# Retention in chunks of 128 rows and FFN tiles of 512 tokens, in place of 96 and 384

## The chip, the cores and the metric

The kernel runs on one NeuronCore of a Trainium2 chip. The metric is the device time of one launch in microseconds (us); lower is better. A core has five engines that run side by side and wait for one another through semaphores: TensorE (PE in the profile; PEld are its weight loads), VectorE (DVE), ScalarE (ACT), GpSimd (POOL) and SyncE (SP), which here only issues loads.

## What is computed

The inputs q, k and v have 8 batches of 8 heads, 576 positions and 64 features. Retention is causal linear attention with a decay gamma that differs by head. Its output, 4608 tokens of 512 features, goes through a feed-forward network (FFN) that takes the greatest of three products and then multiplies once more. All of it is float32.

```python
scores = scale * np.matmul(q, k.transpose(0, 1, 3, 2))
gamma = 1.0 - 2.0 ** (-5.0 - np.arange(H, dtype=np.float32))
Dmat = np.where(rel >= 0, gamma[:, None, None] ** rel[None, :, :], 0.0)
attn_out = np.matmul(scores * Dmat[None, :, :, :], v)
x = attn_out.transpose(0, 2, 1, 3).reshape(B * S, H * D)     # 4608 x 512
h = np.maximum(np.maximum(x @ w1, x @ w2), x @ w3)           # 4608 x 768
return h @ w_out                                             # 4608 x 512
```

## The kernel before

Retention works on chunks of C = 96 positions of one batch, all 8 heads at once: 6 chunks to a sequence of 576, 48 chunks in all. A head's 64 features fill half of the 128 partitions, so heads go in 4 pairs. One chunk g is worked on in three steps, each of which is a "slot" of the main loop:

- `transposes(g)`: 4 transposes of the decayed keys (tile `kt`) and 4 of the queries (`qt`), copied to SBUF by DVE (`kT`) and ACT (`qT`).
- `scores(g)`: 8 products of keys and queries (tile `s`), one for each head, two of them at a time on the two halves of the array's rows; DVE multiplies them by the causal mask (`st`). Then 4 products `kv`, keys by values with 128 columns for a pair of heads, which DVE adds to the running state (`ssum`) and POOL multiplies by the decay (`state`). The last chunk of a sequence has no `kv`, since nothing follows it.
- `values(g)`: 8 products of the values and `st` (tile `o`), two at a time on the two halves of the array's columns, and 4 products of the state and the queries (`o<-qT,state`), which the first chunk of a sequence does without. DVE multiplies the sum by the output's decay and writes it into `xT`, feature-major.

In float32 each product other than a transpose is two MATMUL instructions in the trace. POOL multiplies the keys of chunk g by their decay in `decay_keys(g)` (tile `kd`), two chunks ahead; SP loads k, q and v of a chunk four chunks ahead (`load`).

The FFN works on tiles of NT = 4 C = 384 tokens, 12 tiles in all, one tile behind the retention. Its pieces of work are called atoms: 18 `up` (three weights by six blocks of 128 hidden features; each is four products of 128x128 weights with `NT` columns) and NT / 128 `down` (128 tokens by 512 features; six products of 512 columns). ACT copies the first of three `up` results into `h`, DVE takes the maximum with the others; ACT copies `down` into `osb` and issues the store.

What sets the order is the program text: each engine runs its instructions in the order in which the loop issues them. After each slot, as many atoms are issued as a credit allows, so that the atoms of one tile spread evenly over the 12 slots of the next tile's four chunks:

```python
slots_per_tile = 3 * CPT
atoms_per_tile = 3 * NF + NT // P
def slot(fn):
    fn()
    if todo:
        credit += atoms_per_tile
    while todo and credit >= slots_per_tile:
        credit -= slots_per_tile
        atom()
```

With CPT = 4 chunks to a tile, the FFN of the first tile is queued when `values(3)` has been issued; until then PE has retention alone. The weights arrive as the bits of float64 numbers and have to be converted: 24 pieces, each with five instructions on DVE (`expo`, `expo`, `frac`, `mant`, `expo`), two on ACT and one on POOL. Four pieces are converted beside chunks 0 and 1. The other 20 are issued two at a time ahead of each of the first ten atoms, so that on DVE two conversions stand ahead of whatever follows the atom's products. The products of `up` and `down` share two PSUM buffers, so `up` number n + 2 waits until ACT or DVE has read number n.

Of the kernel before, what the change touches and what calls it, by code (L numbers as in the profile page):

```python
"""Retention (decayed causal linear attention), then a maxout FFN, in float32.

Retention runs over chunks of C positions.  With positions counted within a chunk,
gamma^(i-j) = gamma^i * gamma^-j, so the keys carry gamma^-j, the outputs gamma^i / sqrt(D),
and what earlier chunks add is their state: S' = gamma^C * (S + K'^T V).  Its output comes out
feature-major, as the FFN's first products take it.  The FFN runs on tiles of NT tokens, each
while the retention of the next tile is worked out.
"""
# [10 lines left out]
FP32 = mybir.dt.float32  # L19
# [4 lines left out]
ALU = mybir.AluOpType  # L24
PSUM = bass.MemoryType.PSUM

C = 96
NT = 4 * C
AHEAD = 4
WAHEAD = 4  # L30
# [3 lines left out]
def kernel(  # L34
# [14 lines left out]
    nc = tc.nc  # L49
    P = 128  # L50
    B, H, S, D = q.shape
    N, DM = out.shape
    DF = moe_w1.shape[1]
    NP = H // 2
    NCH = S // C
    NG = B * NCH
    NDC = DM // P
    NF = DF // P
    CPT = NT // C
    assert S % C == 0 and N % NT == 0 and NT % P == 0 and 2 * D == P and NP == NDC  # L60

    const = ctx.enter_context(tc.tile_pool(name="const", bufs=1))
    wraw = ctx.enter_context(tc.tile_pool(name="wraw", bufs=WAHEAD))
# [2 lines left out]
    kpool = ctx.enter_context(tc.tile_pool(name="kpool", bufs=4))  # L66
    att = ctx.enter_context(tc.tile_pool(name="att", bufs=3))
    stp = ctx.enter_context(tc.tile_pool(name="stp", bufs=3))
    xpool = ctx.enter_context(tc.tile_pool(name="xpool", bufs=3))
    hpool = ctx.enter_context(tc.tile_pool(name="hpool", bufs=2))  # L70
    opool = ctx.enter_context(tc.tile_pool(name="opool", bufs=4))
    ps_t = ctx.enter_context(tc.tile_pool(name="ps_t", bufs=1, space=PSUM))
    ps_s = ctx.enter_context(tc.tile_pool(name="ps_s", bufs=1, space=PSUM))
    ps_o = ctx.enter_context(tc.tile_pool(name="ps_o", bufs=1, space=PSUM))
# [13 lines left out]
    causal = const.tile([C, C], FP32, name="causal")  # L88
# [1 line left out]
    nc.gpsimd.affine_select(out=causal[:], in_=causal[:], compare_op=ALU.is_ge, fill=0.0,  # L90
                            base=0, channel_multiplier=-1, pattern=[[1, C]])

# [1 line left out]
    raws, kds, qks, sts, states = {}, {}, {}, {}, {}  # L94

    def load(g):
        b, c = divmod(g, NCH)
        for n, src in (("k", k), ("q", q), ("v", v)):
            t = raws[n, g] = raw.tile([C, H, D], FP32, tag=n, name=n + "raw")
            nc.sync.dma_start(t[:], src[b, :, c * C:(c + 1) * C, :].rearrange("h p d -> p h d"))  # L100

    def decay_keys(g):
        t = kds[g] = kpool.tile([C, H, D], FP32, tag="kd", name="kd")
        nc.gpsimd.tensor_tensor(t[:], raws.pop(("k", g))[:], gk[:].unsqueeze(2).to_broadcast([C, H, D]),  # L104
                                op=ALU.mult)

    def pair(t, p):
        return t[:, 2 * p:2 * p + 2, :].rearrange("a h d -> a (h d)")

    def transposes(g):  # L110
        both = {}
        for n, src in (("k", kds[g]), ("q", raws.pop(("q", g)))):
            pt = ps_t.tile([P, NP, C], FP32, tag=n + "t", name=n + "t")
            for p in range(NP):
                nc.tensor.transpose(pt[:, p, :], pair(src, p), ident[:C, :C])  # L115
            t = both[n] = att.tile([P, NP, C], FP32, tag=n + "T", name=n + "T")
            if n == "k":
                nc.vector.tensor_copy(t[:], pt[:])  # L118
            else:
                nc.scalar.copy(t[:], pt[:])  # L120
        qks[g] = both

    def scores(g):
        c = g % NCH
        qT, kT = qks[g]["q"], qks[g]["k"]
        s = [ps_s.tile([C, NP, C], FP32, tag=f"s{j}", name=f"s{j}") for j in range(2)]
        for p in range(NP):
            for j in range(2):
                r = slice(D * j, D * (j + 1))
                nc.tensor.matmul(s[j][:, p, :], lhsT=kT[r, p, :], rhs=qT[r, p, :], start=True, stop=True)  # L130
        st = sts[g] = att.tile([C, 2, NP, C], FP32, tag="st", name="st")
        for j in range(2):
            nc.vector.tensor_tensor(st[:, j], s[j][:], causal[:].unsqueeze(1).to_broadcast([C, NP, C]),  # L133
                                    op=ALU.mult)
        kd = kds.pop(g)
        if c == NCH - 1:
            return
        kv = ps_kv.tile([P, NP, P], FP32, tag="kv", name="kv")
        for p in range(NP):
            nc.tensor.matmul(kv[:, p, :], lhsT=pair(kd, p), rhs=pair(raws["v", g], p), start=True, stop=True)  # L140
        t = states[g + 1] = stp.tile([P, NP, P], FP32, tag="state", name="state")
        if c == 0:
            nc.vector.tensor_tensor(t[:], kv[:], gs[:], op=ALU.mult)
        else:
            u = stp.tile([P, NP, P], FP32, tag="sum", name="ssum")
            nc.vector.tensor_tensor(u[:], kv[:], states[g][:], op=ALU.add)  # L146
            nc.gpsimd.tensor_tensor(t[:], u[:], gs[:], op=ALU.mult)  # L147
# [1 line left out]
    xT = {}  # L149

    def values(g):
        c = g % NCH
        t, i = divmod(g, CPT)
        if i == 0:
            xT[t] = xpool.tile([P, NDC, NT], FP32, tag="xT", name="xT")
        st, vr, qT = sts.pop(g), raws.pop(("v", g)), qks.pop(g)["q"]
        o = ps_o.tile([P, NP, C], FP32, tag="o", name="o")
        for p in range(NP):
            for j in range(2):
                nc.tensor.matmul(o[D * j:D * (j + 1), p, :], lhsT=vr[:, 2 * p + j, :], rhs=st[:, j, p, :],  # L160
                                 start=(p == 0), stop=(c == 0 and p == NP - 1), skip_group_check=True)
        if c > 0:
            sd = states.pop(g)
            for p in range(NP):
                nc.tensor.matmul(o[:, p, :], lhsT=sd[:, p, :], rhs=qT[:, p, :],  # L165
                                 start=False, stop=(p == NP - 1), skip_group_check=True)
        nc.vector.tensor_tensor(xT[t][:, :, i * C:(i + 1) * C], o[:], gq[:], op=ALU.mult)  # L167

# [1 line left out]
    # The weights come as the bits of float64 numbers, high word (sign, 11 bits of exponent, 20 of  # L170
    # mantissa) and low word (32 of mantissa).  As float32, rounded once:
    #   sign 2^(e - 1023) * ((1 + low 2^-52) + high's mantissa 2^-20),
    # with the exponent clamped to float32's, 0 below and infinity above.
    one = const.tile([P, 1], FP32, name="one")
    nc.vector.memset(one[:], 1.0)
    rebias = const.tile([P, 1], FP32, name="rebias")
# [4 lines left out]
    w_sb, bits = {}, {}  # L181
# [60 lines left out]
    def push_ffn(t):  # L242
        h = hpool.tile([P, NF, NT], FP32, tag="h", name="h")
        for fb in range(NF):
            for i in range(3):
                todo.append(lambda fb=fb, i=i: up(t, h, fb, i))
        for m in range(NT // P):
            todo.append(lambda m=m: down(t, h, m))

# [1 line left out]
    slots_per_tile = 3 * CPT  # L251
    atoms_per_tile = 3 * NF + NT // P
    credit = 0
# [1 line left out]
    def slot(fn):  # L255
        nonlocal credit
# [6 lines that stand above are left out]
# [9 lines left out]
    for g in range(2, AHEAD):  # L272
        load(g)
    decay_keys(0)
    decay_keys(1)
    transposes(0)
    for g in range(NG + 1):
        if g + AHEAD < NG:
            load(g + AHEAD)
        if g + 2 < NG:  # L280
            decay_keys(g + 2)
        if g + 1 < NG:
            slot(lambda: transposes(g + 1))
        if g > 0:
            slot(lambda: values(g - 1))
            if g % CPT == 0:
                push_ffn(g // CPT - 1)
        if g < NG:
            slot(lambda: scores(g))
        if g < 2:  # L290
            next_weights(2)
# [7 lines left out]


def _decays(H, D):
    """The decays of a chunk of C positions, constants of the shapes: for the keys [C, H], the outputs
    [2 D, H / 2, C] and the states [2 D, H / 2, 2 D], two heads to a block of the diagonal."""
    import numpy as _np

    gamma = 1.0 - 2.0 ** (-5.0 - _np.arange(H))
    pos = _np.arange(C)
    keys = gamma[None, :] ** -pos[:, None]
    outs = (gamma[:, None] ** pos[None, :] / math.sqrt(D)).reshape(H // 2, 2, C)
    outs = _np.repeat(outs.transpose(1, 0, 2), D, axis=0)  # L310
    states = _np.zeros((2, D, H // 2, 2, D))
    for j in range(2):
        states[j, :, :, j, :] = (gamma[j::2] ** C)[None, :, None]
    states = states.reshape(2 * D, H // 2, 2 * D)
    return {n: _np.ascontiguousarray(a, dtype=_np.float32)
            for n, a in (("key_decay", keys), ("out_decay", outs), ("state_decay", states))}
# [28 lines left out]
```

## Time and profile before

| what | value |
|---|---|
| three runs | 1023.16 us median, 1019.09 to 1024.40 |
| span of the profiled execution, first to last instruction | 1022.5 us |
| instructions | 11136 |
| granted TensorE clock, mean | 0.985 |
| DMA traffic | 51.51 MB |

The time that belongs to the profiled execution alone isn't listed; its span lies 0.7 us below the median of the runs, and that difference stands here for what lies around a span. The profile's page divides the span into 40 slices, lists groups of instructions by line and tile, and follows the chain of work that ended last back from the end. In a timeline, a row that ends in x16 is a run of 16 like instructions; since matmuls overlap and their ends are modelled, what one matmul costs is read from the distance between starts, not from its duration.

### The profile page before, as it was taken

How to read it: one execution, taken by the hardware profiler on the slowest of the kernel's cores; microseconds unless marked ns; L12 is line 12 of the kernel's file. 1: busy time of each engine (PE TensorE's matmuls, PEld its weight loads, DVE VectorE, ACT ScalarE, POOL GpSimd, SP SyncE). 2: the span in 40 equal slices, each digit the busy share in tenths (PEclk: the TensorE clock that was granted, in tenths of full speed). 3: DMA queues.
4: the chain of work that ended last, by engine and by line, in shares of the span. 5: the costliest groups of instructions: out<-in, count | busy, mean ns of one | idle time of the engine just before them, and what ended most of it. 6: DMA issues, size and time to landing. Idle time of an engine off the chain costs nothing.

```text
span 1022.5 us, 11136 instructions
## 1 busy us (share of the span) xinstructions
PE 977.8 (96%) x4720; PEld 596.4 (58%) x4720; DVE 284.8 (28%) x498; ACT 112.2 (11%) x205; POOL 122.4 (12%) x112
## 2 busy tenths in 40 slices
PE   5976599999999999999999999999999999999998
PEld 4843365665665665665665665665566566565554
DVE  4599921221221221220221221221222121121010
ACT  2133301001000000000100000000100100100100
POOL 2343310010010100110000100110010100000000
PEclk9988799999999999999999999999999999999999
DMA  9744612212212112121112112112112200000000
GB/s 234 157 126 146 142 24 55 47 24 54 47 24 54 33 39 54 24 47 44 35 40 50 35 25 56 44 24 57 44 24 44 57 8 9 24 1 1 31 1 31
DMA packets 128897, 51.51 MB, mean 50 GB/s; under 512 B 114000, under 2 KB 123344, under 8 KB 128848
## 3 DMA queue, kind: packets, MB, share of 16 engines
q1 hardware_dynamic: 123264, 40.91, 18.3%
q10 hardware_dynamic: 5584, 9.90, 3.0%
q8 instruction: 37, 0.61, 0.3%
q14 instruction: 12, 0.10, 0.0%
HBM read 41.36 MB, written 9.44 MB: 50 GB/s over the span
## 4 chain that ended last, share of the span: by engine, by line
PE 90%; DVE 7%; DMA 1%; SPq 1%; issue 1%; POOL 0%; ACT 0%; DVEq 0%
PE up L226 52%; PE down L236 18%; PE kv L140 4%; PE o L165 4%; PE s L130 4%; PE o L160 4%; DVE expo L203 2%; PE kt L115 2%; PE qt L115 1%; DVE expo L210 1%; DVE expo L202 1%; DVE mant L208 1%; DMA kraw<-in_k_dram 1%; DVE frac L207 1%; SPq L100 1%
## 5 line engine op out<-in xcount | busy, mean ns | idle before, releaser
L226 PE MATMUL up<-xT,w 128*128 128x384 f32 x1728 | 593.4, 496 | 27.1 <-DVE h L231 19.3
L226 PEld LDWEIGHTS up<-xT,w 128*128 128x128 f32 x1728 | 323.4, 193 | 233.4 <-issue 34.2
L231 DVE TENSOR_TENSOR h<-h,up 128x384 f32<-128x384 f32 x144 | 79.7, 554 | 401.6 <-PE up L226 396.7
L236 PE MATMUL down<-wout,h 128*128 128x512 f32 x432 | 189.3, 593 | 0.0
L236 PEld LDWEIGHTS down<-wout,h 128*128 128x128 f32 x432 | 81.3, 190 | 96.0 <-issue 92.8
L147 POOL TENSOR_TENSOR state<-ssum,gs 128x512 f32<-128x512 f32 x32 | 40.7, 1273 | 728.9 <-DVE ssum L146 721.9
L133 DVE TENSOR_TENSOR st<-s,causal 96x384 f32<-96x384 f32 x96 | 48.9, 548 | 143.8 <-PE s L130 143.8
L229 ACT COPY h<-up 128x384 f32<-128x384 f32 x72 | 34.4, 478 | 495.5 <-PE up L226 493.5
L167 DVE TENSOR_TENSOR xT<-o,gq 128x384 f32<-128x384 f32 x48 | 26.7, 556 | 105.1 <-PE o L165 103.5
L130 PEld LDWEIGHTS s<-qT,kT 64*96 64x96 f32 x768 | 39.6, 173 | 27.1 <-issue 27.1
L104 POOL TENSOR_TENSOR kd<-kraw,gk 96x512 f32<-96x512 f32 x48 | 50.0, 1052 | 13.9 <-DMA kraw<-in_k_dram 13.9
L160 PEld LDWEIGHTS o<-st,vraw 96*64 96x64 f32 x768 | 35.5, 144 | 27.0 <-issue 18.7
L140 PE MATMUL kv<-vraw,kd 96*128 96x128 f32 x320 | 50.9, 307 | 0.0
L165 PE MATMUL o<-qT,state 128*128 128x96 f32 x320 | 47.9, 296 | 0.0
L130 PE MATMUL s<-qT,kT 64*96 64x96 f32 x768 | 47.9, 268 | 0.0
L239 ACT COPY osb<-down 128x512 f32<-128x512 f32 x36 | 21.1, 586 | 220.5 <-PE down L236 220.5
L140 PEld LDWEIGHTS kv<-vraw,kd 96*128 96x128 f32 x320 | 42.8, 208 | 4.1 <-issue 0.9
L160 PE MATMUL o<-st,vraw 96*64 96x96 f32 x768 | 45.0, 262 | 0.0
L165 PEld LDWEIGHTS o<-qT,state 128*128 128x128 f32 x320 | 41.2, 201 | 5.0 <-issue 0.7
L118 DVE COPY kT<-kt 128x384 f32<-128x384 f32 x48 | 26.6, 554 | 56.9 <-PE kt L115 56.8
L115 PEld LDWEIGHTS kt<-ident,kd 96*128 96x128 f32 x192 | 23.1, 153 | 28.9 <-POOL kd L104 15.2
L115 PE MATMUL kt<-ident,kd 96*128 96x96 f32 x192 | 26.5, 264 | 14.0 <-POOL kd L104 14.0
(25 smaller groups left out, 251.8 us busy)
## 6 DMA issues: line engine op xcount, KB each, us to landing
kraw<-in_k_dram SPq DMA_DIRECT2D x48, 192.0 KB, 3.9
qraw<-in_q_dram SPq DMA_DIRECT2D x48, 192.0 KB, 4.1
vraw<-in_v_dram SPq DMA_DIRECT2D x48, 192.0 KB, 3.3
bits<-in_moe_w_dram SPq DMA_DIRECT2D x18, 512.0 KB, 3.8
out_dram<-osb ACTq DMA_DIRECT2D x36, 256.0 KB, 2.0
bits<-in_moe_w_out_dram SPq DMA_DIRECT2D x6, 512.0 KB, 3.5
gs<-in_state_decay_dram ACTq DMA_DIRECT2D x1, 256.0 KB, 5.3
gq<-in_out_decay_dram ACTq DMA_DIRECT2D x1, 192.0 KB, 4.1
```

Of the source, the lines that this page charges most:

```text
L104: nc.gpsimd.tensor_tensor(t[:], raws.pop(("k", g))[:], gk[:].unsqueeze(2).to_broadcast([C, H, D]), op=ALU.mult)
L115: nc.tensor.transpose(pt[:, p, :], pair(src, p), ident[:C, :C])
L130: nc.tensor.matmul(s[j][:, p, :], lhsT=kT[r, p, :], rhs=qT[r, p, :], start=True, stop=True)
L133: nc.vector.tensor_tensor(st[:, j], s[j][:], causal[:].unsqueeze(1).to_broadcast([C, NP, C]), op=ALU.mult)
L140: nc.tensor.matmul(kv[:, p, :], lhsT=pair(kd, p), rhs=pair(raws["v", g], p), start=True, stop=True)
L147: nc.gpsimd.tensor_tensor(t[:], u[:], gs[:], op=ALU.mult)
L160: nc.tensor.matmul(o[D * j:D * (j + 1), p, :], lhsT=vr[:, 2 * p + j, :], rhs=st[:, j, p, :], start=(p == 0), stop=(c == 0 and p == NP - 1) ...
L165: nc.tensor.matmul(o[:, p, :], lhsT=sd[:, p, :], rhs=qT[:, p, :], start=False, stop=(p == NP - 1), skip_group_check=True)
L226: nc.tensor.matmul(ps[:, 0:NT], lhsT=w_sb[i, fb][:, dc * P:(dc + 1) * P], rhs=xT[t][:, dc, :], start=(dc == 0), stop=(dc == NDC - 1))
L229: nc.scalar.copy(h[:, fb, :], ps[:, 0:NT])
L231: nc.vector.tensor_tensor(h[:, fb, :], h[:, fb, :], ps[:, 0:NT], op=ALU.max)
L236: nc.tensor.matmul(ps[:], lhsT=h[:, fb, m * P:(m + 1) * P], rhs=w_sb["out", fb][:], start=(fb == 0), stop=(fb == NF - 1))
```

## The change

C becomes 128, and with it NT = 4 C becomes 512: 36 chunks and 9 FFN tiles. 576 is 4.5 times 128, so chunks are now counted over (batch, position) as one row of 4608, and of every nine chunks the fifth holds the last 64 positions of one sequence and the first 64 of the next. For such a chunk each of its three loads is two DMAs of 64 partitions; a second mask (`causal64`, shown as `causal_116` below) also clears the products between the two sequences; `kv` uses only the rows of the new sequence, and its state starts afresh; the old state goes into the first 64 columns of `o` alone. Four chunks have no `kv` and four have no old state, in place of eight and eight. The pool for `xT` goes from three buffers to two, that for `osb` from four to three. `atoms_per_tile` goes from 21 to 22 with the fourth `down`. Comments are taken out.

```diff
-C = 96
+C = 128
 NT = 4 * C
...
-    NCH = S // C
-    NG = B * NCH
+    NG = B * S // C
...
-    xpool = ctx.enter_context(tc.tile_pool(name="xpool", bufs=3))
+    xpool = ctx.enter_context(tc.tile_pool(name="xpool", bufs=2))
...
-    opool = ctx.enter_context(tc.tile_pool(name="opool", bufs=4))
+    opool = ctx.enter_context(tc.tile_pool(name="opool", bufs=3))
...
+    def start_of(g):
+        r = -g * C % S
+        return r if r < C else None
+
+    masks = {0: causal, None: causal}
+    for r in sorted({start_of(g) for g in range(NG)} - {0, None}):
+        m = masks[r] = const.tile([C, C], FP32, name=f"causal{r}")
+        nc.gpsimd.tensor_copy(m[:], causal[:])
+        nc.gpsimd.memset(m[0:r, r:C], 0.0)
...
-            nc.sync.dma_start(t[:], src[b, :, c * C:(c + 1) * C, :].rearrange("h p d -> p h d"))
+            row = 0
+            while row < C:
+                b, pos = divmod(g * C + row, S)
+                n = min(C - row, S - pos)
+                nc.sync.dma_start(t[row:row + n], src[b, :, pos:pos + n, :].rearrange("h p d -> p h d"))
+                row += n
...
-        if c == NCH - 1:
+        if g + 1 == NG or start_of(g + 1) == 0:
             return
+        r = start_of(g) or 0
...
-            nc.tensor.matmul(kv[:, p, :], lhsT=pair(kd, p), rhs=pair(raws["v", g], p), start=True, stop=True)
+            nc.tensor.matmul(kv[:, p, :], lhsT=pair(kd, p)[r:], rhs=pair(raws["v", g], p)[r:], start=True, stop=True)
...
-        if c == 0:
+        if start_of(g) is not None:
             nc.vector.tensor_tensor(t[:], kv[:], gs[:], op=ALU.mult)
...
+        old = C if start_of(g) is None else start_of(g)
...
-                nc.tensor.matmul(o[:, p, :], lhsT=sd[:, p, :], rhs=qT[:, p, :],
+                nc.tensor.matmul(o[:, p, :old], lhsT=sd[:, p, :], rhs=qT[:, p, :old],
```

Three places in the order of the instructions matter. The first is PE at the start of the FFN: from the `kv` of chunk 4 to the ups of the first tile. Before:

```order
L140 MATMUL kv<-vraw,kd 128x128 x4
L226 MATMUL up<-xT,w_0_222 128x384 x4
L115 MATMUL kt<-ident,kd 128x96 x4
L115 MATMUL qt<-ident,qraw 128x96 x4
L226 MATMUL up<-xT,w_0_236 128x384 x4
L226 MATMUL up<-xT,w_0_305 128x384 x4
L160 MATMUL o<-st,vraw 64x96 x8
L165 MATMUL o<-qT,state 128x96 x4
```

And now:

```order
L155 MATMUL kv<-vraw,kd 128x128 x4
L241 MATMUL up<-xT,w_0_228 128x512 x4
L130 MATMUL kt<-ident,kd 128x128 x4
L130 MATMUL qt<-ident,qraw 128x128 x4
L241 MATMUL up<-xT,w_0_242 128x512 x4
L241 MATMUL up<-xT,w_0_311 128x512 x4
L175 MATMUL o<-st,vraw 64x128 x8
L180 MATMUL o<-qT,state 128x64 x4
```

The first tile's ups still begin behind the `kv` of chunk 4 and alternate with the same slots; nothing moved, but each `up` is 512 columns wide, and the old state enters 64 columns of chunk 4, which holds two sequences.

The second place is PE behind the scores of chunk 5. Before, it is the last of its sequence:

```order
L130 MATMUL s_705<-qT,kT 96x96
L130 MATMUL s_706<-qT,kT 96x96
L226 MATMUL up<-xT,w_1_522 128x384 x4
L226 MATMUL up<-xT,w_2_564 128x384 x4
L115 MATMUL kt<-ident,kd 128x96 x4
```

And now it has a successor in its sequence:

```order
L144 MATMUL s_709<-qT,kT 128x128
L144 MATMUL s_710<-qT,kT 128x128
L155 MATMUL kv<-vraw,kd 128x128 x4
L241 MATMUL up<-xT,w_1_526 128x512 x4
L241 MATMUL up<-xT,w_2_568 128x512 x4
L130 MATMUL kt<-ident,kd 128x128 x4
```

A `kv` stands there that wasn't there, with a state behind it on DVE and POOL, inside the stretch in which the weights are converted.

The third place is SP's queue in the start, from the loads of chunk 3 to the next weights. Before:

```order
L100 DMA vraw<-in_v_dram 96x8x64
L100 DMA kraw<-in_k_dram 96x8x64
L100 DMA qraw<-in_q_dram 96x8x64
L100 DMA vraw<-in_v_dram 96x8x64
L192 DMA bits<-in_moe_w_dram 128x4x128 x2
```

And now:

```order
L114 DMA vraw<-in_v_dram 128x8x64
L114 DMA kraw<-in_k_dram 64x8x64 x2
L114 DMA qraw<-in_q_dram 64x8x64 x2
L114 DMA vraw<-in_v_dram 64x8x64 x2
L207 DMA bits<-in_moe_w_dram 128x4x128 x2
```

The queue's order is the same; each load is a third larger, and the three of chunk 4 come in two halves.

More of the change, by code (lines that the diff above doesn't have):

```diff
@@ L59 @@
     CPT = NT // C
-    assert S % C == 0 and N % NT == 0 and NT % P == 0 and 2 * D == P and NP == NDC
+    assert B * S % C == 0 and S >= C and N % NT == 0 and NT % P == 0 and 2 * D == P and NP == NDC
     const = ctx.enter_context(tc.tile_pool(name="const", bufs=1))
@@ L91 @@
                             base=0, channel_multiplier=-1, pattern=[[1, C]])
+    def start_of(g):
[6 more added lines that the diff above has]
+        nc.gpsimd.memset(m[0:r, r:C], 0.0)
     raws, kds, qks, sts, states = {}, {}, {}, {}, {}
     def load(g):
-        b, c = divmod(g, NCH)
         for n, src in (("k", k), ("q", q), ("v", v)):
             t = raws[n, g] = raw.tile([C, H, D], FP32, tag=n, name=n + "raw")
-            nc.sync.dma_start(t[:], src[b, :, c * C:(c + 1) * C, :].rearrange("h p d -> p h d"))
+            row = 0
[4 more added lines that the diff above has]
+                row += n
     def decay_keys(g):
@@ L123, in scores @@
     def scores(g):
-        c = g % NCH
         qT, kT = qks[g]["q"], qks[g]["k"]
@@ L132, in scores @@
         for j in range(2):
-            nc.vector.tensor_tensor(st[:, j], s[j][:], causal[:].unsqueeze(1).to_broadcast([C, NP, C]),
+            nc.vector.tensor_tensor(st[:, j], s[j][:], masks[start_of(g)][:].unsqueeze(1).to_broadcast([C, NP, C]),
                                     op=ALU.mult)
         kd = kds.pop(g)
-        if c == NCH - 1:
+        if g + 1 == NG or start_of(g + 1) == 0:
             return
+        r = start_of(g) or 0
         kv = ps_kv.tile([P, NP, P], FP32, tag="kv", name="kv")
         for p in range(NP):
-            nc.tensor.matmul(kv[:, p, :], lhsT=pair(kd, p), rhs=pair(raws["v", g], p), start=True, stop=True)
+            nc.tensor.matmul(kv[:, p, :], lhsT=pair(kd, p)[r:], rhs=pair(raws["v", g], p)[r:], start=True, stop=True)
         t = states[g + 1] = stp.tile([P, NP, P], FP32, tag="state", name="state")
-        if c == 0:
+        if start_of(g) is not None:
             nc.vector.tensor_tensor(t[:], kv[:], gs[:], op=ALU.mult)
@@ L151, in values @@
     def values(g):
-        c = g % NCH
+        old = C if start_of(g) is None else start_of(g)
         t, i = divmod(g, CPT)
@@ L160, in values @@
                 nc.tensor.matmul(o[D * j:D * (j + 1), p, :], lhsT=vr[:, 2 * p + j, :], rhs=st[:, j, p, :],
-                                 start=(p == 0), stop=(c == 0 and p == NP - 1), skip_group_check=True)
-        if c > 0:
+                                 start=(p == 0), stop=(old == 0 and p == NP - 1), skip_group_check=True)
+        if old > 0:
             sd = states.pop(g)
             for p in range(NP):
-                nc.tensor.matmul(o[:, p, :], lhsT=sd[:, p, :], rhs=qT[:, p, :],
+                nc.tensor.matmul(o[:, p, :old], lhsT=sd[:, p, :], rhs=qT[:, p, :old],
                                  start=False, stop=(p == NP - 1), skip_group_check=True)
```

## Prediction

> **What bounds the kernel now.** The page's busy times come first, then its slices and the chain that ended last.
>
> ```profile
> PE 977.8 (96%) x4720; PEld 596.4 (58%) x4720; DVE 284.8 (28%) x498; ACT 112.2 (11%) x205; POOL 122.4 (12%) x112
> PE   5976599999999999999999999999999999999998
> DVE  4599921221221221220221221221222121121010
> PE 90%; DVE 7%; DMA 1%; SPq 1%; issue 1%; POOL 0%; ACT 0%; DVEq 0%
> ```
>
> TensorE sets the end from the sixth slice on; in the slices before it VectorE is full while TensorE has gaps. The sums by stage make that exact (columns: stretch and length, busy us of PE, PEld, DVE, ACT and POOL with counts, granted clock, DMA share, GB/s).
>
> ```profile
> 0.00:52.30 52.30, 38.30 (x257) 33.66 (x258) 25.84 (x46) 10.11 (x16) 17.61 (x22) 1.00 0.93 191
> 52.30:127.00 74.70, 47.64 (x194) 27.38 (x194) 71.63 (x113) 29.18 (x45) 29.08 (x22) 0.83 0.54 142
> 182.00:1018.90 836.90, 836.88 (x4020) 503.14 (x4018) 175.16 (x317) 67.66 (x134) 68.88 (x62) 1.00 0.15 34
> ```
>
> There are three regimes. Up to 52.3 us there is retention alone, with the DMA engines at 0.93. Up to 127 us VectorE converts weights (71.63 of 74.70 us busy) and TensorE follows. From 182 us on TensorE never pauses, at full clock, so there a change is worth exactly what it takes from TensorE's stream of instructions.
>
> **TensorE's stream, priced.** A timeline of the steady part, where distances between starts are costs:
>
> ```profile
> 526.25 0.50 PE L115 MATMUL kt<-ident,kd 96*128 96x96 f32 x4
> 526.59 0.49 PE L115 MATMUL qt<-ident,qraw 96*128 96x96 f32 x4
> 526.92 5.35 PE L226 MATMUL up<-xT,w 128*128 128x384 f32 x16
> 532.20 0.88 PE L160 MATMUL o<-st,vraw 96*64 96x96 f32 x16
> 533.01 1.13 PE L165 MATMUL o<-qT,state 128*128 128x96 f32 x8
> 533.98 2.77 PE L226 MATMUL up<-xT,w 128*128 128x384 f32 x8
> 536.68 0.92 PE L130 MATMUL s<-qT,kT 64*96 64x96 f32 x16
> 537.53 1.16 PE L140 MATMUL kv<-vraw,kd 96*128 96x128 f32 x8
> 538.53 5.33 PE L226 MATMUL up<-xT,w 128*128 128x384 f32 x16
> 543.69 0.49 PE L115 MATMUL kt<-ident,kd 96*128 96x96 f32 x4
> ...
> 553.98 10.49 PE L236 MATMUL down<-wout,h 128*128 128x512 f32 x24
> 564.41 0.92 PE L130 MATMUL s<-qT,kT 64*96 64x96 f32 x16
> ```
>
> Sixteen ups of 384 columns take 543.69 - 538.53 = 5.16 us, 0.3225 each. Sixteen that stand between transposes and `o` take 5.28: 0.12 us is lost in the two switches around them; the ups before `s` show it again (2.70 for eight, not 2.58). So a chunk loses 0.24 us in switches. A down of 512 columns takes (10.43 - 0.12) / 24 = 0.4295. Between the two widths a column costs (0.4295 - 0.3225) / 128 = 0.84 ns, and next to nothing is fixed.
>
> Ups: 1728 x 0.3225 = 557.3 us now, 1296 x 0.4295 = 556.6 then. The wider tile gains 0.7 us by itself; the downs stay the same.
>
> ```profile
> L226 PE MATMUL up<-xT,w 128*128 128x384 f32 x1728 | 593.4, 496 | 27.1 <-DVE h L231 19.3
> L140 PE MATMUL kv<-vraw,kd 96*128 96x128 f32 x320 | 50.9, 307 | 0.0
> L165 PE MATMUL o<-qT,state 128*128 128x96 f32 x320 | 47.9, 296 | 0.0
> L165 PEld LDWEIGHTS o<-qT,state 128*128 128x128 f32 x320 | 41.2, 201 | 5.0 <-issue 0.7
> L160 PEld LDWEIGHTS o<-st,vraw 96*64 96x64 f32 x768 | 35.5, 144 | 27.0 <-issue 18.7
> ```
>
> Retention, for a chunk: transposes 526.92 - 526.25 = 0.67, `o` 0.81, `s` 0.85, switches 0.24, together 2.57; `kv` 1.00; the state's products 0.97. Of these, transposes (8), `s` (8 pairs) and `o` (8 pairs) stream C columns each, so 32 more columns add 24 x 32 x 0.84 ns = 0.64 us: 3.21. `kv` streams 128 columns whatever C is. The state's products stream C columns, yet with 96 they already cost as much as `kv` with 128: both load 128 columns of weights, and that load (201 ns, against 144 for 64 columns) sets their pace. With 128 columns they can cost from 0.97 to `kv`'s 1.00, or (8 x 32 x 0.84 ns added in full) 1.19; I take 0.97, since `kv` is the same shape.
>
> - Chunks: 48 x 2.57 - 36 x 3.21 = 123.4 - 115.6 = 7.8 us less.
> - `kv`: 40 chunks become 32, 8 x 1.00 = 8.0 less.
> - State's products: likewise 8 x 0.97 = 7.8 less (2 if 1.19 holds).
>
> With the ups, TensorE's stream is 24.3 us shorter. The second DMA of a crossing chunk, the second mask and the 64-partition loads cost nothing: loads lie behind a DMA share of 0.15. By the Trainium skill's page "DMA: Bandwidth & Descriptors" a transfer in two partition halves gains nothing and a single one should be used; by it the four split chunks pay only queue time, which that share hides.
>
> The smaller pools cost nothing either: `o` of the tile after next is issued only when the tile's last downs have been, so two `xT` suffice, and an `osb` comes back after a copy and a store of 2.0 us, while three downs of 6 x 2 x 0.43 = 5.2 us each pass:
>
> ```profile
> out_dram<-osb ACTq DMA_DIRECT2D x36, 256.0 KB, 2.0
> L231 DVE TENSOR_TENSOR h<-h,up 128x384 f32<-128x384 f32 x144 | 79.7, 554 | 401.6 <-PE up L226 396.7
> L146 DVE TENSOR_TENSOR ssum<-kv,state 128x512 f32<-128x512 f32 x32 | 22.1, 691 | 6.2 <-PE kv L140 2.8
> ```
>
> An up's read grows from 0.55 to about 0.69 us on VectorE (the price of a 512-wide read), beside an up of 8 x 0.43 = 3.4 us: hidden.
>
> **The start** (rows of POOL's and PE's timelines):
>
> ```profile
> 17.82 1.22 POOL L104 TENSOR_TENSOR kd<-kraw,gk 96x512 f32<-96x512 f32 x1 [6.67 <-DMA kraw<-in_k_dram]
> 35.74 0.90 PE L115 MATMUL kt<-ident,kd 96*128 96x96 f32 x4 [1.16 <-POOL kd L104]
> 36.43 0.85 PE L115 MATMUL qt<-ident,qraw 96*128 96x96 f32 x4
> 44.04 0.85 PE L115 MATMUL kt<-ident,kd 96*128 96x96 f32 x4
> 52.28 3.74 PE L226 MATMUL up<-xT,w 128*128 128x384 f32 x8
> GB/s 234 157 126 146 142 24 55 47 24 54 47 24 54 33 39 54 24 47 44 35 40 50 35 25 56 44 24 57 44 24 44 57 8 9 24 1 1 31 1 31
> ```
>
> Chunk 2's keys land at 17.82 behind the loads of chunks 0 and 1, four weight pieces and the constants; chunks that are a third larger and the wider constants put 0.5 MB more ahead, at 234 GB/s 2.2 us. From there to the first up at 52.28, TensorE runs at half speed (four transposes in 36.43 - 35.74 = 0.69, against 0.34 later), so a chunk's 0.64 us is 1.28, and three of them lie on the path (chunk 1, and the two iterations from 35.74 and 44.04 on): 3.9. VectorE's wider reads add some 0.4 between 17.8 and 35.7. First up at 52.3 + 6.5 = 58.8. Of that 3.2 us is retention work done (6 transposes, 5 `s`, 4 `o`, at 8 x 32 x 0.84 ns each); the start loses 3.3 us.
>
> **The conversions.** Both kernels issue 20 conversions ahead of ten atoms; VectorE's order holds each up's read behind them.
>
> ```profile
> 113.16 5.46 PE L226 MATMUL up<-xT,w 128*128 128x384 f32 x8 [6.28 <-DVE h L231]
> 118.55 1.19 PE L130 MATMUL s<-qT,kT 64*96 64x96 f32 x16
> 119.67 1.16 PE L140 MATMUL kv<-vraw,kd 96*128 96x128 f32 x8
> 120.66 2.75 PE L226 MATMUL up<-xT,w 128*128 128x384 f32 x8
> 126.68 5.46 PE L226 MATMUL up<-xT,w 128*128 128x384 f32 x8 [3.27 <-ACT h L229]
> 131.93 0.85 PE L115 MATMUL kt<-ident,kd 96*128 96x96 f32 x4
> ```
>
> From the first up to the last wait at 126.68, eleven ups pass in 74.4 us; the wait is for VectorE, so this stretch takes what VectorE takes. Its 13 or so wider reads add 13 x 0.14 = 1.8, and the `ssum` of chunk 5, which is new there, 0.6: 2.4 us longer. In it TensorE does more: 11 ups x 8 x 0.107 = 9.4, wider retention in six slots 1.3, chunk 5's `kv` 1.0, together 11.7, all in gaps like the 6.28 us above. That brings forward 11.7 - 2.4 = 9.3 us.
>
> The sum: 1022.5 - 24.3 + 3.3 - 9.3 = 992.2 us of span; with the 0.7 between span and median, **992.9 us**.
>
> **Rivals.**
>
> The start grows as the chunk does. If the stretch before the first up, with its DMA engines at 0.93, grows by a full third, 52.3 becomes 69.7 and not 58.8: 10.9 more, **1003.8**. Against it, VectorE's conversions of the first four pieces stand in that stretch and don't grow.
>
> The clock stays up. The up at 113.16, behind a gap of 6.28 us, takes 5.39 us to the next row and the one at 120.66 only 2.7: long gaps are followed by half speed. The one at 126.68 runs at half speed too (131.93 - 126.68 = 5.25, against 2.6), and from there on TensorE is the bound, so 2.6 us of it and 0.5 of the transposes count. If fuller gaps keep the clock up, 3.1 us go: **989.8**. The Trainium skill's page "TensorE: Matmul & The Clock Gate" (Part 1) has half rate follow an idle window of about 3.4 us, which free-running windows place by chance; by it shorter gaps would save those 3.1 us. The trace agrees only in part: a gap of 3.27 us still ended in half speed.
>
> Pairs fall apart: the slower side. `s` and `o` run two products side by side: eight pairs of `o` in 0.81 us, where 16 single ones at a `kt`'s 0.083 would take 1.3. If full 128-wide `s` tiles or 128-row `o` tiles no longer overlapped, each of 36 x 16 = 576 pairs would cost about 0.107 more: 61.6 us, **1054.5**. It decides from 0.05 us a pair on, where it eats the 30 us gained. Against it: what pairs are halves of 64 rows or 64 columns, and those stay.
>
> A pool too small. If `xT` or `osb` were waited for at each of 8 tile boundaries, for half a down, 1.3 us, it would cost 10 us: **1003**; the order and the 2.0 us of a store speak against it.
>
> **How the numbers follow.** Forecast 0.66 (by itself 987 to 999: the state's products at 1.19 add 6, the start may be 5 better or worse); start by a third 0.15; clock kept 0.12; pool 0.04; pairs 0.03. From 983 (clock kept and a start that doesn't grow) to 1004 holds all but the pairs and a tail on either side. A measurement of this kernel can tell about 0.5% from no change, that is 5 us: all cases but the pairs are faster by more; I leave 0.03 for no change, where several small losses would meet, and 0.03 for slower.
>
> **What would show it.** In the profile after: sixteen ups in 6.87 us; `s` to `kv` in about 1.07; the state's products still near 0.97; first up near 59 us, last wait near 135; no PE idle time behind `xT` or `osb` in the steady part. An `o` group of 1.6 us or more would show the pairs apart; PE gaps after 190 us would make the forecast wrong; a first up at 65 us or later, the first rival.

## The result, and the profile after

The changed kernel takes 980.95 us in the median of four runs (980.17 to 981.67), against 1022.09 (1019.09 to 1024.40) for the kernel before: a ratio of 0.9597, 95% interval 0.9571 to 0.9622. The prediction was 992.9 us with a range of 983 to 1004. The direction was right, the gain of 41 us was put at 30, and the measured time lies 2 us below the range.

The spans of the two profiled executions are 1022.5 and 978.6 us, 43.9 apart. Part of the difference to the 41 is that the profile of before is of a long run; another profile of the same kernel (e6 below) has a span of 1019.5. What lies around a span is 1.7 us in these two kernels (980.29 with 978.6, 1021.23 with 1019.5), not the 0.7 that was taken.

The page after, by the same lines as before:

```profile
PE 936.9 (96%) x3680; PEld 484.0 (49%) x3680; DVE 264.0 (27%) x406; ACT 107.3 (11%) x175; POOL 100.6 (10%) x94
PE   4787699999999999999999999999999999999998
DVE  3799931122112221222122202221122112210110
```

TensorE has gaps in the first five slices, as before, but a slice is 24.5 us long now, not 25.6, and VectorE is full in the third to the fifth of them in both. The sums by stage after, cut at the first up (49.1) and at TensorE's last wait (118.6); columns as before:

```profile
0.00:49.10 49.10, 30.38 (x256) 25.99 (x256) 27.73 (x46) 10.76 (x16) 17.99 (x24) 0.93 1.13 236
49.10:118.60 69.50, 50.14 (x171) 24.13 (x169) 67.00 (x105) 27.24 (x41) 27.05 (x21) 0.90 0.62 166
182.00:974.90 792.90, 792.90 (x3012) 401.52 (x3010) 151.41 (x228) 61.45 (x105) 45.78 (x41) 1.00 0.14 32
```

The three regimes are the same, and the steady one still has no gap. The steady part of TensorE's timeline after:

```profile
129.41 0.60 PE L130 MATMUL kt<-ident,kd 128*128 128x128 f32 x4
130.28 7.03 PE L241 MATMUL up<-xT,w 128*128 128x512 f32 x16
137.24 1.09 PE L175 MATMUL o<-st,vraw 128*64 128x128 f32 x16
138.27 1.16 PE L180 MATMUL o<-qT,state 128*128 128x128 f32 x8
139.26 7.03 PE L241 MATMUL up<-xT,w 128*128 128x512 f32 x16
146.22 1.16 PE L144 MATMUL s<-qT,kT 64*128 64x128 f32 x16
147.32 1.16 PE L155 MATMUL kv<-vraw,kd 128*128 128x128 f32 x8
148.31 7.03 PE L241 MATMUL up<-xT,w 128*128 128x512 f32 x16
155.18 0.60 PE L130 MATMUL kt<-ident,kd 128*128 128x128 f32 x4
```

Sixteen ups take 155.18 - 148.31 = 6.87 us, as predicted. A chunk's transposes take 0.87, `o` 1.03, `s` 1.10, the two switches 0.18: 3.18 (predicted 3.21); `kv` and the state's products 0.99 each. The stream is 36 x 3.18 + 32 x (0.99 + 0.99) + 1296 x 0.4294 + 432 x 0.4295 = 919.9 us; by the same sum with the numbers of before 123.4 + 40.0 + 38.8 + 557.3 + 185.5 = 945.0. So the stream lost 25.1 us (predicted 24.3), and the remaining 43.9 - 25.1 = 18.8 came from the first 130 us, where 6.0 had been expected.

Where in them? Before its first up at 52.28 the old kernel had done 6 x 0.67 + 4 x 0.81 + 5 x 0.85 + 5 x 1.00 + 3 x 0.97 = 19.4 us of the stream, so 32.9 us were lost there. The new one has its first up at 49.15 with 22.8 us done by the same count: 26.4 lost. **The start gained 6.5 us where a loss of 3.3 was predicted.**

The other 12.3 us have two parts. From the first up to the twelfth the old kernel took 126.68 - 52.28 = 74.40 us and did 36.46 of the stream (eleven ups 28.38, retention 8.08), the new one 125.97 - 49.15 = 76.82 us and 48.06 (37.79 and 10.27): 37.94 us lost before, 28.76 after. So the conversions gained 9.2 us, where 9.3 was predicted. The last 3.0 us lie at the twelfth up itself: in the profile of before it and the transposes behind it ran at half speed, in the profile after they didn't.

The start after, from the transposes of chunk 4 on, which began at 35.74 before:

```profile
37.35 1.11 PE L130 MATMUL kt<-ident,kd 128*128 128x128 f32 x4 [4.57 <-DVE st L147]
38.26 1.06 PE L130 MATMUL qt<-ident,qraw 128*128 128x128 f32 x4
39.25 1.74 PE L175 MATMUL o<-st,vraw 128*64 128x128 f32 x16
40.91 1.16 PE L180 MATMUL o<-qT,state 128*128 128x128 f32 x8
42.00 1.16 PE L144 MATMUL s<-qT,kT 64*128 64x128 f32 x16
44.09 0.60 PE L130 MATMUL kt<-ident,kd 128*128 128x128 f32 x4
44.53 0.60 PE L130 MATMUL qt<-ident,qraw 128*128 128x128 f32 x4
49.15 3.70 PE L241 MATMUL up<-xT,w 128*128 128x512 f32 x8
```

Four transposes take 38.26 - 37.35 = 0.91 us in the first iteration and 0.44 in the second: the clock rose in between, near 40.6 us. (It had been up before, in the iteration from 27.40 on, and fallen in the wait of 4.57 us.) Before, it stayed at half through both iterations, which took 16.5 us; now, with more work in them, they take 11.8. The clock column doesn't show this for the kernel before, since the record of the clock begins with its first change, at 54.30 us: the row 0.00:52.30 of before says 1.00 for a stretch that the spacing of every instruction shows to be at half speed.

### The profile page after: what moved, and what is told of

Same layout as the page of the kernel before. It is cut to its first block, busy times and chain, and to the rows that moved or that the text cites. A ratio compares the mean times of both kernels' runs of the same rounds, so it can differ in the third digit from the quotient of the medians.

```text
span 978.6 us, 8776 instructions
## 1 busy us (share of the span) xinstructions
PE 936.9 (96%) x3680; PEld 484.0 (49%) x3680; DVE 264.0 (27%) x406; ACT 107.3 (11%) x175; POOL 100.6 (10%) x94
## 3 DMA queue, kind: packets, MB, share of 16 engines
q1 hardware_dynamic: 122880, 40.90, 19.4%
## 4 chain that ended last, share of the span: by engine, by line
PE 89%; DVE 8%; issue 1%; DMA 1%; SPq 0%; POOL 0%; ACT 0%; DVEq 0%
PE up L241 54%; PE down L251 19%; PE s L144 4%; PE o L175 3%; PE o L180 3%; PE kv L155 3%; DVE expo L218 2%; PE kt L130 2%; DVE expo L225 2%; PE qt L130 1%; DVE expo L217 1%; DVE mant L223 1%; DVE frac L222 1%; DMA kraw<-in_k_dram 1%; DVE st L147 0%
## 5 line engine op out<-in xcount | busy, mean ns | idle before, releaser
L241 PE MATMUL up<-xT,w 128*128 128x512 f32 x1296 | 579.4, 600 | 19.4 <-DVE h L246 16.5
L241 PEld LDWEIGHTS up<-xT,w 128*128 128x128 f32 x1296 | 242.5, 192 | 298.9 <-issue 295.3
L246 DVE TENSOR_TENSOR h<-h,up 128x512 f32<-128x512 f32 x108 | 74.2, 687 | 400.3 <-PE up L241 400.3
L147 DVE TENSOR_TENSOR st<-s,causal 128x512 f32<-128x512 f32 x72 | 46.4, 685 | 109.9 <-PE s L144 109.9
L144 PEld LDWEIGHTS s<-qT,kT 64*128 64x128 f32 x576 | 35.8, 191 | 24.4 <-issue 24.0
L144 PE MATMUL s<-qT,kT 64*128 64x128 f32 x576 | 42.8, 289 | 0.0
L175 PE MATMUL o<-st,vraw 128*64 128x128 f32 x576 | 40.6, 285 | 0.0
L119 POOL TENSOR_TENSOR kd<-kraw,gk 128x512 f32<-128x512 f32 x36 | 37.6, 1054 | 14.7 <-DMA kraw<-in_k_dram 14.7
L155 PE MATMUL kv<-vraw,kd 128*128 128x128 f32 (+1 forms) x256 | 36.9, 287 | 0.0
L180 PE MATMUL o<-qT,state 128*128 128x128 f32 (+1 forms) x256 | 36.9, 287 | 0.0
L130 PEld LDWEIGHTS kt<-ident,kd 128*128 128x128 f32 x144 | 18.7, 148 | 34.7 <-POOL kd L119 18.8
```

The source lines that it names most:

```text
L147: nc.vector.tensor_tensor(st[:, j], s[j][:], masks[start_of(g)][:].unsqueeze(1).to_broadcast([C, NP, C]), op=ALU.mult)
L155: nc.tensor.matmul(kv[:, p, :], lhsT=pair(kd, p)[r:], rhs=pair(raws["v", g], p)[r:], start=True, stop=True)
L180: nc.tensor.matmul(o[:, p, :old], lhsT=sd[:, p, :], rhs=qT[:, p, :old], start=False, stop=(p == NP - 1), skip_group_check=True)
L241: nc.tensor.matmul(ps[:, 0:NT], lhsT=w_sb[i, fb][:, dc * P:(dc + 1) * P], rhs=xT[t][:, dc, :], start=(dc == 0), stop=(dc == NDC - 1))
L246: nc.vector.tensor_tensor(h[:, fb, :], h[:, fb, :], ps[:, 0:NT], op=ALU.max)
```

## The experiments

Three questions: is the clock what shortened the start, and what raised it; what share has the wide tile; and does the loss in the conversions come from what stands ahead in VectorE's queue.

**e1: array use.** A first theory was that 96 of 128 rows and columns are too little use of the array for the clock to rise.

```diff
+KR = 96
...
-                nc.tensor.matmul(s[j][:, p, :], lhsT=kT[r, p, :], rhs=qT[r, p, :], start=True, stop=True)
+                nc.tensor.matmul(s[j][0:KR, p, :], lhsT=kT[r, p, 0:KR], rhs=qT[r, p, :], start=True, stop=True)
...
-                nc.tensor.matmul(o[D * j:D * (j + 1), p, :], lhsT=vr[:, 2 * p + j, :], rhs=st[:, j, p, :],
+                nc.tensor.matmul(o[D * j:D * (j + 1), p, :], lhsT=vr[0:KR, 2 * p + j, :], rhs=st[0:KR, j, p, :],
...
```

> The changed kernel with 96 of 128 rows or columns of the array in use in four of the five kinds of retention products (kv, o and the state's products contract 96 rows; s makes 96 output columns); the transposes stay whole. It leaves out the last 32 keys and values of each chunk and 32 rows of each state. The instructions, their widths and so their full-speed cost stay. Theory A, array use (the clock rose in the start because 128 rows by 128 columns are in use, where 96 did not raise it): half speed until the first up, first up at 56 to 59 us in place of 49, time 988 to 991 us. Rival B (the clock rose because a burst happened to cover a window of the gate): nothing changes, first up at 49 us, time 979 to 983. Rival C (the start is shorter for another reason than the clock): first up at 49 us whatever the clock shows.

980.85 us (980.27 to 981.04), span 978.6, first up at 50.08, with the clock up at the same places as in the changed kernel. Array use is not it; theory A fell.

**e2: the chunk alone.** `NT = 3 * C`, so that chunks of 128 feed tiles of 384.

> Chunks of 128 with FFN tiles of three chunks, 384 tokens, as wide as before the change. The full-speed stream is 0.8 us longer than the changed kernel's. Theory (the wider tile pays by giving TensorE more work per up while VectorE converts weights): 11 ups of 2.58 in place of 3.43 us leave 9 to 10 us more of gaps in the conversions, the first up comes one chunk earlier, near 42 us, which returns 2 or 3 us of it: 986 to 991 us. Rival (the whole gain is the chunk's, the tile's width gives nothing): 978 to 982 us.

992.28 us (991.32 to 992.91), ratio 0.9715 (0.9693 to 0.9737). The chunk alone gains 30 us, the wide tile the other 11.3, 1.3 more than the range expected, and it gains it in the conversions, as TensorE's timeline of e2 shows:

```profile
45.88 5.33 PE L241 MATMUL up<-xT,w 128*128 128x384 f32 x16
61.30 5.49 PE L241 MATMUL up<-xT,w 128*128 128x384 f32 x8 [5.18 <-DVE h L246]
75.63 2.82 PE L241 MATMUL up<-xT,w 128*128 128x384 f32 x8 [3.40 <-ACT h L244]
84.01 4.48 PE L241 MATMUL up<-xT,w 128*128 128x384 f32 x8 [5.56 <-DVE h L246]
```

The first up comes 3.3 us earlier than with 512 (a chunk less ahead of it), and yet gaps of over 5 us are back, as before the change.

**e3 and e9: the kernel before with its waits filled.** Extra products of the identity with itself stand ahead of the transposes of chunks 1 to 4, where TensorE waits: 12, 8, 4 and 4 products in e3, 16, 20, 16 and 20 in e9.

```diff
+        warm(WARM.get(g, 0))
         if g + 1 < NG:
             slot(lambda: transposes(g + 1))
```

> The kernel before, with 12, 8, 4 and 4 extra products of the identity with itself (128 rows, columns and moving columns) on TensorE ahead of the transposes of chunks 1, 2, 3 and 4, where it waits for POOL. Theory A (the start before is paced by a TensorE at half speed): the clock rises near 10 to 17 us, the stretch from 35.7 us to the first up takes some 9 in place of 16.5 us, first up at 44 to 46, time 1014 to 1017 us. If three quarters of the array do not hold the clock up either, it drops again and only part of this shows, 1018 to 1021. Rival C (the clock does not pace the start): first up at 52 us or later, 1022 us or more.

e3 gave 1021.57 us (1016.42 to 1023.53, ten runs), ratio 0.999 (0.9971 to 1.001): no measurable gain. Its profile is of a run of 1017.33 us; there the first up came at 45.70 and the span was 1015.6, but the clock had fallen and risen twice on the way. This settled nothing for the other runs, so e9 filled the waits whole.

> The kernel before with 16, 20, 16 and 20 extra products of the identity ahead of the transposes of chunks 1 to 4, so that TensorE's waits of the start are filled up to the first up. Theory (the start before is 6 to 7 us longer than it need be because TensorE runs it at half speed): the clock rises near 10 us and stays up, the first up comes at 44 to 47 in place of 52 us, in every run, 1014 to 1018 us. Rival (the clock is not what sets the first up; loads and VectorE are): first up at 50 us or later, 1020 us or more.

1014.24 us, all six runs within 1012.91 to 1014.58, ratio 0.9927 (0.9899 to 0.9954). TensorE's timeline of e9:

```profile
14.41 4.63 PE L102 MATMUL warm<-ident 128*128 128x128 f32 x40
35.11 0.50 PE L124 MATMUL kt<-ident,kd 96*128 96x96 f32 x4
35.44 0.49 PE L124 MATMUL qt<-ident,qraw 96*128 96x96 f32 x4
44.06 2.75 PE L235 MATMUL up<-xT,w 128*128 128x384 f32 x8
```

Four transposes take 0.33 us, and the first up comes at 44.06, 8.2 us earlier, though TensorE has more to do. So the clock did set the pace of the start before: from 35 us to the first up 9.0 us at full speed, 16.5 at half.

**e4 and e5: which products raise the clock.** Blocks of like products ahead of the kernel before, each but the first behind some 10 us of idle TensorE.

> The kernel before behind six blocks of like products, each block behind some 9 us in which TensorE is idle. Each block is 44 float32 products (88 instructions) of 128 moving columns, some 19 us at half speed: 96 rows by 128 columns of the array; 128 by 128; 128 rows by 96 columns; 112 by 128; 128 by 128 with 96 moving columns; and 11 products of 96 by 128 with 512 moving columns. Theory A: distances between starts stay near 213 ns through the blocks of 96 rows or 96 columns, and halve to about 110 ns within 7 us in the block of 128 by 128; 112 rows may go either way. Rival B: every block that lasts over 7 us rises to full speed alike.

Every block rose. In TensorE's timeline the starts of a block are 213 ns apart at first and 111 later; 88 instructions would last 18.8 us at the one and 9.8 at the other, and all are in between, whatever rows and columns they use:

```profile
3.84 12.25 PE L277 MATMUL probe<-buf 96*128 96x128 f32 x88 [3.84 <-DMA buf<-in_q_dram]
27.46 12.38 PE L277 MATMUL probe<-buf 128*128 128x128 f32 x88 [11.37 <-DVE buf L281]
97.50 13.14 PE L277 MATMUL probe<-buf 128*128 128x96 f32 x88 [10.65 <-DVE buf L281]
```

> The kernel before behind six blocks of products without any wait inside, each behind some 9 us in which TensorE is idle: three times a chunk's mix of products as before the change (8 transposes of 96, 8 paired o, 4 of the state, 8 paired s, 4 kv, all 96 wide but kv); paired s of 96 alone; paired o of 96 alone; transposes of 96 alone; the mix with 128 throughout; the mix of 96 again. Theory A2 (some form of the 96-wide mix does not count as work for the clock's gate): the block of the mix of 96 stays at half speed through its 24 us, and one of the blocks of a single form does too; the mix of 128 rises within 8 us. Rival B2 (the form does not matter; what kept the clock down before lies in the waits between the forms, or in when they fall): all six rise within 8 us of their start.

Each of the three forms alone rose. The mix of 96 did so once early and once only at its end, in the same program. Rows of the first, fourth, fifth and sixth blocks of TensorE's timeline:

```profile
4.00 1.51 PE L298 MATMUL pt<-ident,buf 96*128 96x96 f32 x8 [4.00 <-DMA buf<-in_q_dram]
10.40 1.16 PE L304 MATMUL pm<-buf 96*128 96x128 f32 x8
...
73.53 11.94 PE L298 MATMUL pt<-ident,buf 96*128 96x96 f32 x112 [10.59 <-DVE buf L277]
96.14 1.94 PE L298 MATMUL pt<-ident,buf 128*128 128x128 f32 x8 [10.67 <-DVE buf L277]
99.58 1.16 PE L304 MATMUL pm<-buf 128*128 128x128 f32 x8
...
138.57 2.07 PE L304 MATMUL pm<-buf 96*128 96x128 f32 x8
145.29 1.60 PE L284 MATMUL ps<-buf 64*96 64x96 f32 x16
```

The eight products of `kv`'s shape take 1.16 us (full speed) at 10.40, 6 us into the first block, and 2.07 (half) at 138.57, in a block that began at 123.92 and stayed at half speed for 23 us without a pause. The mix of 128 was up some 3 us after it began. So the mix of a 96-wide chunk can run for 6 or for 23 us before the clock rises. Neither A2 nor B2 holds as it was put: none of the forms that were run alone keeps the clock down, and a clock that stays down needs no waits.

**e6: the kernel before, once more.**

> The kernel before, once more, for a second profile of its start. If the half speed up to 54 us is a property of the kernel: no rise of the clock before the first up at 52 us. If it is chance: a rise somewhere between 16 and 45 us, the first up 3 to 7 us earlier and the span shorter by as much.

1021.23 us, span 1019.5: half speed up to the first up at 52.35 again. The span is 3.0 us shorter for another reason, as TensorE's timeline of e6 shows at the twelfth up:

```profile
126.75 2.82 PE L226 MATMUL up<-xT,w 128*128 128x384 f32 x8 [3.40 <-ACT h L229]
129.41 0.49 PE L115 MATMUL kt<-ident,kd 96*128 96x96 f32 x4
```

It took 2.66 us to the next row here and 5.25 in the first profile, and the transposes behind it ran at full speed too. So the 3.0 us that the changed kernel saved there need not be the change's: the same kernel loses them in one execution and not in another.

**e12: the kernel before with streams of 128 columns in its start.**

```diff
+def width(g):
+    return 128 if g < 6 else C
...
-        s = [ps_s.tile([C, NP, C], ...
+        W = width(g)
+        s = [ps_s.tile([C, NP, W], ...
```

> The kernel before with s, o and the state's products of chunks 0 to 5 streaming 128 columns (32 of them zeros that nothing reads) in place of 96, all else as before but two buffers for xT. Theory W (with streams of 128 columns the clock rises in the start, with 96 it mostly does not): a rise between 16 and 30 us, the first up at 45 to 49 us although each chunk streams more, 1016 to 1021 us. Rival (the width of the streams is not it): half speed up to the first up, which comes at 54 to 57 us, 1024 to 1028 us.

1019.15 us (1018.25 to 1022.5, ten runs), ratio 0.9981 (0.9961 to 1.0000). The profile has theory W's rise, between the scores and `kv` of chunk 1, and then the first up 2.6 us earlier though each chunk streams more:

```profile
15.60 2.08 PE L150 MATMUL kv<-vraw,kd 96*128 96x128 f32 x8
25.49 1.21 PE L150 MATMUL kv<-vraw,kd 96*128 96x128 f32 x8
49.65 2.75 PE L236 MATMUL up<-xT,w 128*128 128x384 f32 x8
```

The first up is 0.65 us later than the theory's range, since the clock fell once more in the wait ahead of 37.31 and rose again near 42.7. Six chunks' extra columns eat most of the gain, so the time alone would not have decided, and this is one profile; with 49.65 against 49.15 in the changed kernel the starts are alike.

**e7, e8 and e10: one conversion ahead of an up.** The edit of e7 and e8:

```diff
     def atom():
-        next_weights(2)
+        next_weights(2 if len(w_sb) < 6 else 1)
         todo.popleft()()
```

> The changed kernel with one conversion ahead of each up in place of two, as soon as six pieces are there. Theory (from the first up on, TensorE waits for reads that VectorE has queued behind two conversions): VectorE's work is the same, but 20 ups pass beside it in place of ten, so that TensorE has some 87 us of work in a stretch of some 92 in place of 41 in 69: 20 us fewer gaps, 958 to 966 us. Rival (the gaps come from the weights arriving late, or from the total of VectorE's work): under 5 us, 976 to 984 us.

954.76 us (954.66 to 958.09), ratio to the kernel before 0.9342 (0.932 to 0.9363): **26 us faster than the changed kernel**, the fastest of all, and more than expected. The sums by stage of e7, cut at the first up and behind the first downs:

```profile
49.60:140.00 90.40, 88.35 (x345) 45.41 (x344) 80.71 (x130) 32.58 (x50) 36.59 (x29) 1.00 0.56 141
```

VectorE is still busy for 80.71 us, but TensorE is too for 88.35 of 90.40, and without gaps its clock is at 1.00 there, not 0.90. The loss in the conversions was the order of VectorE's queue.

> The kernel before with one conversion ahead of each up in place of two. If the wide tile's gain lies in the conversions, narrow ups fill the stretch less well: 20 ups of 2.58 us and 4 chunks make 69 us of work in some 90 of VectorE's, so 18 us fewer gaps, 1002 to 1008 us, and about 4 us less gained than with wide ups. Rival: as much gained as in the changed kernel.

1006.29 us (1002.97 to 1007.36), ratio 0.9829 (0.9808 to 0.985): 16 us gained with the narrow ups, 26 with the wide ones, a difference of 10 where 4 was expected.

> The changed kernel with one conversion ahead of each up, and with two pieces in place of four converted beside chunks 0 and 1 (the two left over are caught up with later, one at every sixth piece). Theory (from 16 to 38 us VectorE's uninterrupted row sets the pace of the start, and four conversions are 14 us of it): the first up comes 4 to 7 us earlier than at 49.7, 948 to 952 us. Rival (the loads set the pace there): first up at 48 us or later, 953 to 957 us.

958.72 us (958.13 to 959.43): 4 us slower than e7. The first up came 6 us earlier, and more than that was given back:

```profile
43.62 3.70 PE L241 MATMUL up<-xT,w 128*128 128x512 f32 x8
89.63 5.12 PE L241 MATMUL up<-xT,w 128*128 128x512 f32 x8 [3.03 <-DVE h L246]
136.26 7.97 PE L251 MATMUL down<-wout,h 128*128 128x512 f32 x14 [3.41 <-POOL wout L228]
```

The theory of the start was right, but its 948 to 952 us were missed: the conversions taken out of the start came back as waits at 89.63 and, for the last weights, at 136.26. VectorE was busy for 86.76 of the 93.40 us from 43.60 to 137.00, so its total is the likely limit there; no run tested that.

**e11: the smaller pools.** The kernel before with `bufs=2` for `xT` and `bufs=3` for `osb`.

> The kernel before with the smaller pools of the changed one, two buffers for xT and three for osb. The prediction had them cost nothing: within 2 us of the kernel before. If xT or osb were waited for at the tile boundaries: 8 us or more longer.

1023.20 us, ratio 1.0015 (0.9995 to 1.0036): nothing, as predicted.

## Why the prediction was off

- **TensorE's stream** was right: 25.1 us less for 24.3. The state's products cost 0.99 us with 128 columns, 0.97 with 96 and 0.94 with the 64 of a crossing chunk (62.06 to 63.00 in e7), so their columns hardly count; that fits the weight load as their pace. The wide ups gain under 1 us in the steady part.
- **The pools, the split loads and wider reads** cost nothing (e11; no gap from 182 us on). The rivals of the pairs and the pools didn't occur.
- **The start is the step that failed.** The prediction put it: "From there to the first up at 52.28, TensorE runs at half speed", so "a chunk's 0.64 us is 1.28, and three of them lie on the path", and "First up at 52.3 + 6.5 = 58.8". It was at 49.15. Of the 9.7 us, 2.3 are ahead of chunk 4's transposes: the sum gave 35.74 + 2.2 + 1.3 + 0.4 = 39.6, they began at 37.35, since VectorE's unbroken row of reads and conversions from 16.42 on, with POOL's work behind it, set their time and not TensorE's slowness (in e10, with two conversions fewer in that row, they begin at 33.33; in e7 it was 37.80). The other 7.3 are the two iterations behind them, 11.8 us in place of 16.5 + 2.6 = 19.1: the clock was up in the second and in half of the first. That the clock sets this stretch is shown by e9.
- **What raised the clock** is in part open. That the 128-wide streams do is what e5 and e12 point to. All six profiles with such streams in a kernel's start (after, e1, e2, e7, e10, e12) have the clock up before the first up. By the record of the clock it rose in five of them 3 to 5 us after chunk 4's transposes began (in e10 it had stayed up). With the old start and no extra products inside it, that took 9 to 20 us: in four profiles (before, e4, e6, e11) the clock rose only behind the first up, in e8 1 us and in e5 4 us ahead of it. So the 96-wide start can rise too, late, and what decides when isn't shown.
- **The rival "the clock stays up"** came true where it was priced, 3.0 us for 3.1 behind the last wait. But in e6 it does so without any fuller gap, so chance is enough for it; that the fuller gaps had a part isn't shown. The larger part of half speed, the start, had been taken as given.
- **The conversions** were right, 9.2 us for 9.3, and so was their length: the twelfth up came 76.82 us after the first, 2.4 more than before. That it began at 125.97 and not near 135 is the start alone. TensorE's last wait was at 118.59, before the eleventh up:

```profile
118.59 5.37 PE L241 MATMUL up<-xT,w 128*128 128x512 f32 x8 [3.63 <-DVE h L246]
123.89 1.16 PE L144 MATMUL s<-qT,kT 64*128 64x128 f32 x16
125.97 3.60 PE L241 MATMUL up<-xT,w 128*128 128x512 f32 x8
```

  The twelfth no longer waits, since its predecessor and a chunk's scores cover the read, which ended 0.2 us ahead of it, at 125.74. e2 gives the wide tile's share, 11.3 us, and e7 shows that the cause of the loss that is left is the order of VectorE's queue.
- **In sum**, the spans lie 43.9 us apart and not 30.3. Of the 13.6 between, 9.8 are the start, 3.0 the half speed behind the last wait and 0.8 the stream. The base hid some of it: what lies around a span was taken as 0.7 us and is 1.7.

## What to carry to other kernels

Price a change to a TensorE-bound kernel from the distances between starts in its steady part; that held within 1 us here. One profile is one execution: two of the kernel before differ by 3.0 us, so compare two before what they lose is put into a sum. Where TensorE waits often, first find out at which clock it works there, from the spacing of like instructions and not from the mean clock, and give a rise or a fall of it a term of its own. And look at what stands in an engine's queue ahead of the read that frees a buffer: one conversion fewer ahead of each read was worth more here than the wide tile.

## What the runs showed of the hardware

The clock's rise can't be told from how long TensorE is busy. The Trainium skill's page "TensorE: Matmul & The Clock Gate" (Part 1) has full rate follow one busy window of about 3.4 us; most blocks agree (full speed 3 to 7 us after a block's begin), but the 96-wide mix stayed at half for 23 us in e5 without a pause, and the kernel before for 16.5 us from 35.74 on. Once up, the clock held in the same mix: in e9 the 96-wide chunks ran at full speed from 35.11 us to the first up at 44.06. What raises the clock stays open. The same page (Part 4) says that full rate does not engage for transposes, which do not count as busy in the same way; here a block of 112 transposes alone, which would take 18 us at half speed and 9.2 at full, took 11.94, so it rose within it.

The clock is also a likely part of the spread: the kernel before took 1015 to 1025 us in the 23 runs beside the last four experiments, with its start filled in e9 1012.9 to 1014.6, and the changed kernel 980.2 to 981.7. Two profiles, before and e6, show 3.0 us of it; the rest isn't shown.
